# Stores of the attention rows on ScalarE's queue, loads at the head of a unit into three buffers, decay products ahead of the logits

## The chip, the core and the metric

One Trainium2 chip, one of its cores. The time of a kernel is the device time of one execution in microseconds (us); the median of the runs is compared. The profile names the engines PE (TensorE matmul), PEld (TensorE weight load), DVE (VectorE), ACT (ScalarE), POOL (GpSimd) and SP (SyncE). A name with a q behind it (SPq, ACTq) is that engine's instruction queue where it issues transfers.

## The reference, cut to what matters

Three stages follow one another: a gated recurrent attention, a mixture of experts with a greedy, capped assignment of tokens, and a two-layer network. The change touches the first alone.

```python
for t in range(S):                       # B, H, S, D = 4, 8, 768, 40
    m_new = np.maximum(f_gate[:, :, t] + m, i_gate[:, :, t])
    f_stab = np.exp(f_gate[:, :, t] + m - m_new)
    i_stab = np.exp(i_gate[:, :, t] - m_new)
    C = f_stab[..., None, None] * C + i_stab[..., None, None] * np.einsum('bhd,bhe->bhde', vt, kt)
    n = f_stab[..., None] * n + i_stab[..., None] * kt
    h_tilde = np.einsum('bhde,bhe->bhd', C, qt)
    denom = np.maximum(np.abs(np.einsum('bhd,bhd->bh', n, qt)[..., None]), 1.0)
    y[:, :, t] = h_tilde / denom / (1.0 + np.exp(-o_gate[:, :, t]))
x = y.transpose(0, 2, 1, 3).reshape(B * S, H * D)      # 3072 rows of 320
logits = x @ w_gate                      # then: greedy assignment of 3072 tokens to 8 experts
```

## The kernel before, in words

The sequence of 768 steps is cut into 12 chunks of 64 steps. A chunk holds four batches, taken as two pairs, so that the attention runs in 24 **units**: unit u is chunk n = u // 2 and batch pair bp = u % 2. The 128 partitions are 64 steps of the two batches of a pair. Inside a chunk the recurrence is written as matrix products with decay weights; from chunk to chunk a state (tile C, three buffers per pair) is carried.

For each chunk two transfers bring the inputs: `load_qk` (line 252) brings keys and queries (tile qk, 1 MB) into one of two fixed buffers, chunk n into buffer n % 2, and `load_vk` (line 256) brings values, keys by step and the output gate (tile vk, 968 KB), also into two buffers. Both are issued by SP. SP's queue also holds the stores of finished rows to device memory (xd, two stores of 64 rows for each unit, line 432) and the fetches of pieces of the later stage's weights (cx, line 856). It issues in the order of the program: an instruction that waits holds up all that stand behind it.

`run` (line 456) writes one unit after the other. In unit u, with v = u + 1 and w = u + 2, the work is:

- PE: `values(u)` and `scores(w)` interleaved (lines 368 and 283; the scores read qk of chunk w // 2), `recall(u)` and `state(u)` interleaved (382 and 394), `turn(u - 1)` (438, the transpose of finished rows), `logits(u - 1)` (448, it needs the transposed rows xT that ACT copies at 440), `decay(w)` (291, two times eight products into pF and pD).
- DVE: `scan(v)` (309) and `weigh(v)` (359), the denominators rd of `gates(u)` (414, 416, 418, once recall and state of unit u are done), `add_state(u)` (405), the finished rows x of `rows_out(u)` (427).
- POOL: sg (420, the gate times the reciprocal, it needs DVE's line 418), kt (328) and C (330) of `fade(v)`, vp (316) and qt (319) of `factors(v)`.
- ACT: xT (440), the sigmoid sg (354), the copy db of the second decay product (302), which qt reads, the logits L (449), and the last columns of x (429).

Between these, `fl(i)` puts steps of other work: the conversion of the weight pieces (lines 873 to 938, on ACT, DVE and POOL, from unit 4 on) and the first steps of the assignment of tokens (lines 608 to 628 on DVE, in one unit out of four).

In the kernel before, at the end of an even unit u, behind the stores of that unit, `load_qk` and `load_vk` of chunk u // 2 + 2 are issued. Their keys are first read by `scores` of unit u + 2. The last two units store through ACT's queue, the other 22 through SP's.

Of the kernel before, what the change touches and what calls it, by code (L numbers as in the profile page):

```python
# [8 lines left out]
F32 = mybir.dt.float32  # L9
# [8 lines left out]
NS, NU = 12, 24  # L18
# [16 lines left out]
class Plan:  # L35
# [46 lines left out]
    def next(self):  # L82
        self.due(min(self.todo)[0])
# [30 lines left out]
class Attention:  # L114
# [4 lines left out]
    def __init__(self, nc, tc, consts, qk, vk, ig, fg, wg, xd, L, ident):  # L119
        self.nc, self.tc, self.qk, self.vk, self.xd, self.L, self.ident = nc, tc, qk, vk, xd, L, ident  # L120
        self.es = ExitStack()
        one = self.es.enter_context(tc.tile_pool(name="a1", bufs=1))
# [19 lines left out]
        warm = one.tile([1, 8], F32, name="warm")  # L142
        V.memset(warm, 0.0)
        A.activation(warm, warm, AF.Exp)
        self.QKb = [one.tile([128, 2, 2, 8, 64], F32, name=f"qk{i}") for i in range(2)]
        self.QK, self.VK, self.W = {}, {}, {}
        for bp in range(2):
            self.load_qk(0, bp)
# [101 lines left out]
        self.nc.scalar.activation(self.isT[:, n0:n1].rearrange("p n h -> p (n h)"), self.pG[:, n0 * 16:n1 * 16], AF.Copy)  # L250

    def load_qk(self, n, bp=slice(0, 2)):
        self.QK[n] = self.QKb[n % 2]
        self.nc.sync.dma_start(self.QK[n][:, bp], self.qk[n, :, bp])

    def load_vk(self, n):
        self.VK[n] = self.two.tile([128, 2, 968], F32, name="vk")
        self.nc.sync.dma_start(self.VK[n], self.vk[n])

    def by_token(self, u, i):  # L260
# [161 lines left out]
    def rows_out(self, u):  # L422

        nc = self.nc
        n, bp = divmod(u, 2)
        x = self.st["x", u] = self.two.tile([128, 384], F32, name="x", bufs=3)
        nc.vector.tensor_tensor(x[:, :320].rearrange("p (h d) -> p h d", d=40), self.st.pop(("O", u))[:, :, :40],
                                self.st.pop(("sg", u)), op=ALU.mult)
        nc.scalar.activation(x[:, 320:], x[:, 256:320], AF.Copy)
        for r in range(2):  # L430
            row = (bp * 2 + 1 - r) * S + n * 64
            (nc.scalar if u > NU - 3 else nc.sync).dma_start(self.xd[row:row + 64], x[r * 64:r * 64 + 64])

    def turn(self, u):
        x = self.st.pop(("x", u))
# [20 lines left out]
    def run(self, hook, fill):  # L456
        later = self.later()
        for u in range(NU):
            v, w = u + 1, u + 2
            fl = lambda i: ([fill() for _ in range(FP[i])] if u > FU else []) + [self.step() for _ in range(EP[i])]  # L460
            self.both(self.values(u), self.scores(w))
            self.both(self.recall(u), self.state(u))
            if u > 0:
                self.turn(u - 1)
            if v < NU:
                self.scan(v)
                self.factors(v)
                self.opens(v)
                self.weigh(v)
            fl(0)  # L470
            if u < 3:
                next(later, None)
            self.gates(u, fl)
            if v < NU:
                self.fade(v)
            if u > 0:
                self.logits(u - 1)
            fl(2)
            if w < NU:
                self.decay(w)  # L480
            self.add_state(u)
            fl(3)
            if u == NU - 1:
                while self.extra:
                    self.step()
            self.rows_out(u)
            fl(4)
            if u % 2 == 0 and u // 2 + 2 < NS:
                self.load_qk(u // 2 + 2)
                self.load_vk(u // 2 + 2)  # L490
            if u == 0:
                self.turn_gi(2, NS)
                self.keep_gi(2, NS)
            hook(u)
        self.turn(u)
        self.logits(u)
        hook(NU)
        self.es.close()
# [1011 lines left out]
```

## Time and profile before

| what | value |
|---|---|
| median of 3 runs | 841.85 us (841.56 to 846.75) |
| the profiled execution's own time | 841.95 us |
| its span, first to last instruction | 840.2 us |
| stretch of the attention units (unit 0 to the last transpose) | about 16 to 187 us of the span |
| PE, DVE, ACT, POOL busy in the first 190 us | 132.8, 132.4, 66.9, 117.0 us |
| PE, DVE, ACT, POOL busy in the other 650.2 us | 597.4, 451.8, 282.8, 192.7 us |

The profiled execution lies 0.1 us above the median, and 1.75 us of its time lie outside its span. The share of an engine over the whole span says little here, as the attention and the later stages have different limits; each stage has to be read by itself.

### The profile page before, as it was taken

The numbers are of one execution on the slowest core, as the hardware profiler recorded it, in microseconds if no ns is written. First come the engines' busy times: TensorE is split into PE (matmuls) and PEld (weight loads), VectorE is DVE, ScalarE is ACT, GpSimd is POOL, SyncE is SP. The second block draws the span as 40 slices with busy tenths as digits, with TensorE's granted clock in tenths as the row PEclk, the third lists the DMA queues.
The fourth block names the chain that finished last, engine by engine and source line by source line (L and its number), as shares of the span: only waits on it lengthen the run. The fifth ranks groups of instructions, "written<-read, shape, count | busy, mean of one in ns | idle before, by whom it ended". The sixth has DMA issues, their size and how long they took to land.

```text
span 840.2 us, 18328 instructions
## 1 busy us (share of the span) xinstructions
PE 730.2 (87%) x7355; PEld 679.3 (81%) x7355; DVE 584.1 (70%) x1616; ACT 349.7 (42%) x743; POOL 309.7 (37%) x358
## 2 busy tenths in 40 slices
PE   7776667682889979989999999999999999999995
PEld 5665656571778878878988988899999999999995
DVE  8773776858788996688788778966942862662452
ACT  5322333333526652454354435424633643542431
POOL 3665776743622651352422414410601411211001
PEclk9765988895699989989999999999999999999998
DMA  5565565623520410220310301300310220100000
GB/s 206 182 245 169 164 261 174 221 54 110 181 63 19 149 64 25 84 83 1 128 62 3 112 17 63 104 24 2 128 40 24 91 76 25 63 1 25 1 1 24
DMA packets 20757, 72.79 MB, mean 87 GB/s; under 512 B 3200, under 2 KB 7296, under 8 KB 19264
## 3 DMA queue, kind: packets, MB, share of 16 engines
q1 hardware_dynamic: 11856, 39.41, 13.8%
q0 software_dynamic: 8448, 31.73, 11.4%
q8 instruction: 58, 0.95, 0.5%
q10 hardware_dynamic: 368, 0.49, 0.2%
q14 instruction: 27, 0.22, 0.1%
HBM read 62.96 MB, written 8.65 MB: 85 GB/s over the span
## 4 chain that ended last, share of the span: by engine, by line
PE 52%; DVE 16%; issue 6%; ACT 3%; DMA 0%; POOL 0%; POOLq 0%; ACTq 0%; DVEq 0%
PE ph L1096 24%; PE acc L1234 5%; PE acc L1238 4%; PE acc L1235 4%; PE acc L1203 3%; PE acc L1205 2%; PE acc L1204 2%; DVE e L1149 2%; PE pr L727 2%; DVE gl L980 1%; PE acc L1190 1%; DVE ge L713 1%; PE acc L1192 1%; PE ph L1049 1%; ACT e L1146 1%
## 5 line engine op out<-in xcount | busy, mean ns | idle before, releaser
L1234 PE MATMUL acc<-woh,gh 128*128 128x320 f32 x384 | 123.1, 321 | 0.0
L1238 PE MATMUL acc<-woh,gl 128*128 128x320 f32 x384 | 120.0, 312 | 0.0
L1235 PE MATMUL acc<-wol,gh 128*128 128x320 f32 x384 | 119.4, 311 | 0.0
L1149 DVE SCALAR_TENSOR_TENSOR e<-e,ph 128x384 f32<-128x384 f32 x128 | 69.8, 549 | 61.9 <-ACT e L1146 61.5
L1145 ACT ACTIVATE e<-ph 128x384 f32<-128x384 f32 x128 | 62.6, 489 | 117.4 <-PE ph L1096 113.0
L980 POOL TENSOR_TENSOR gl<-e,gh 128x384 fp32r<-128x384 f32 x33 | 34.4, 1045 | 165.2 <-DVE gh L974 129.9
L1096 PE MATMUL ph<-yh,wih 128*128 128x384 f32 x256 | 90.2, 352 | 0.4
L1096 PE MATMUL ph<-yh,wil 128*128 128x384 f32 x256 | 86.6, 338 | 0.0
L1113 ACT ACTIVATE gh<-ph 128x384 fp32r<-128x384 f32 x64 | 31.3, 491 | 123.0 <-PE ph L1096 121.8
L1244 POOL DMA_INDIRECT out_dram<-ot,idx x24 | 24.0, 998 | 141.3 <-ACT ot L972 138.0
L1120 DVE SCALAR_TENSOR_TENSOR gl<-ph,gh 128x384 fp32r<-128x384 f32 x64 | 35.3, 554 | 56.3 <-ACT gh L1113 55.9
L1238 PEld LDWEIGHTS acc<-woh,gl 128*128 128x128 f32 x384 | 72.8, 190 | 0.6
L1234 PEld LDWEIGHTS acc<-woh,gh 128*128 128x128 f32 x384 | 73.0, 190 | 0.2
L1235 PEld LDWEIGHTS acc<-wol,gh 128*128 128x128 f32 x384 | 73.0, 190 | 0.0
L1146 ACT ACTIVATE e<-e 128x384 f32<-128x384 f32 x128 | 67.3, 526 | 4.0
L1096 PE MATMUL ph<-yl,wih 128*128 128x384 f32 x256 | 66.8, 342 | 0.0
L283 PE MATMUL pS<-qk 64*64 64x64 f32 x768 | 37.5, 268 | 29.5 <-DMA qk<-in_qk_dram 29.5
L283 PEld LDWEIGHTS pS<-qk 64*64 64x64 f32 x768 | 33.5, 177 | 31.4 <-DMA qk<-in_qk_dram 31.4
L980 DVE TENSOR_TENSOR gl<-e,gh 128x384 fp32r<-128x384 f32 x95 | 57.3, 606 | 1.9
L1096 PEld LDWEIGHTS ph<-yh,wih 128*128 128x128 f32 x256 | 48.7, 190 | 4.5 <-ACT yh L1208 4.4
L1096 PEld LDWEIGHTS ph<-yh,wil 128*128 128x128 f32 x256 | 48.6, 190 | 0.0
L1096 PEld LDWEIGHTS ph<-yl,wih 128*128 128x128 f32 x256 | 46.6, 190 | 0.0
(269 smaller groups left out, 2033.2 us busy)
## 6 DMA issues: line engine op xcount, KB each, us to landing
vk<-in_vk_dram SPq DMA_DIRECT2D x12, 968.0 KB, 8.1
qk<-in_qk_dram SPq DMA_DIRECT2D x11, 1024.0 KB, 5.6
wx<-in_wout_dram SPq DMA_DIRECT2D x16, 320.0 KB, 2.8
xd<-x SPq DMA_DIRECT2D x44, 96.0 KB, 3.4
cx<-in_win_dram SPq DMA_DIRECT2D x8, 512.0 KB, 6.8
qk<-in_qk_dram SPq DMA_DIRECT2D x2, 512.0 KB, 5.4
cx<-in_win_dram SPq DMA_DIRECT2D x4, 256.0 KB, 6.2
xd<-x ACTq DMA_DIRECT2D x4, 96.0 KB, 2.2
```

The lines of the kernel that those rows point to most:

```text
L283: self.nc.tensor.matmul(p[r:r + 64, h], k, q, start=True, stop=True)
L980: (self.nc.vector if e == "d" else self.nc.gpsimd).tensor_tensor(out, x, y, op=ALU.subtract)
L1096: PE.matmul(p, w, x, start=k == 0, stop=k == 7)
L1113: nc.scalar.activation(h, p, AF.Relu)
L1120: nc.vector.scalar_tensor_tensor(l, p, 0.0, h, op0=ALU.max, op1=ALU.subtract)
L1145: nc.scalar.activation(e, p, AF.Relu, scale=-1.0)
L1146: nc.scalar.activation(e, e, AF.Exp, scale=-1.0)
L1149: nc.vector.scalar_tensor_tensor(e, e, -1.0, p, op0=ALU.add, op1=ALU.max)
L1203: PE.matmul(p, w[:, c], h, start=f == 0, stop=False)
L1234: PE.matmul(p, h[:, c], self.woh[:, f], start=f == 0, stop=False)
L1235: PE.matmul(p, h[:, c], self.wol[:, f], start=False, stop=False)
L1238: PE.matmul(p, l[:, c], self.woh[:, f], start=False, stop=f == 15)
```

## The change

Three things are done at once.

1. All row stores of the attention are issued by ACT instead of SP (44 of the 48 move; the other four were there).
2. The tiles qk and vk have three buffers, and the loads of chunk u // 2 + 2 are written at the head of the even unit u, ahead of its matmuls, instead of at its end.
3. `decay(w)` is written ahead of `logits(u - 1)`.

```diff
@@ __init__
-        self.QKb = [one.tile([128, 2, 2, 8, 64], F32, name=f"qk{i}") for i in range(2)]
+        self.QKb = [one.tile([128, 2, 2, 8, 64], F32, name=f"qk{i}") for i in range(3)]
@@ load_qk, load_vk
-        self.QK[n] = self.QKb[n % 2]
+        self.QK[n] = self.QKb[n % 3]
-        self.VK[n] = self.two.tile([128, 2, 968], F32, name="vk")
+        self.VK[n] = self.two.tile([128, 2, 968], F32, name="vk", bufs=3)
@@ rows_out
-            (nc.scalar if u > NU - 3 else nc.sync).dma_start(self.xd[row:row + 64], x[r * 64:r * 64 + 64])
+            nc.scalar.dma_start(self.xd[row:row + 64], x[r * 64:r * 64 + 64])
@@ run, for u in range(NU)
+            if u % 2 == 0 and u // 2 + 2 < NS:
+                self.load_qk(u // 2 + 2)
+                self.load_vk(u // 2 + 2)
             self.both(self.values(u), self.scores(w))
...
-            if u > 0:
-                self.logits(u - 1)
             fl(2)
             if w < NU:
                 self.decay(w)
+            if u > 0:
+                self.logits(u - 1)
             self.add_state(u)
...
-            if u % 2 == 0 and u // 2 + 2 < NS:
-                self.load_qk(u // 2 + 2)
-                self.load_vk(u // 2 + 2)
```

How the order of instructions moves at three places:

SP's queue around the loads of two chunks in the middle of the attention (xd is a row store, cx a piece of the later weights). Before:

```order
L254 DMA qk_109<-in_qk_dram 128x2048
L258 DMA vk<-in_vk_dram 128x1936
L856 DMA cx<-in_win_dram 128x1024
L432 DMA xd<-x 64x384 x4
L856 DMA cx<-in_win_dram 128x1024
L254 DMA qk_110<-in_qk_dram 128x2048
L258 DMA vk<-in_vk_dram 128x1936
```

With the change:

```order
L254 DMA qk_111<-in_qk_dram 128x2048
L258 DMA vk<-in_vk_dram 128x1936
L856 DMA cx<-in_win_dram 128x1024
L254 DMA qk_109<-in_qk_dram 128x2048
L258 DMA vk<-in_vk_dram 128x1936
L856 DMA cx<-in_win_dram 128x1024 x2
```

The four stores between two loads are gone from SP's queue, and a third buffer (qk_111) takes its turn; only loads and weight pieces are left.

PE from the transpose of one unit to the first products of the next one (pX holds the transpose and the logits, sel and fp, dp are the decay operands). Before:

```order
L438 MATMUL pX<-ident,x 128x128 x3
L448 MATMUL pX<-wg,xT 128x8 x3
L291 LDWEIGHTS sel
L291 MATMUL pF<-fp,sel 128x64
...
L291 MATMUL pD<-dp,sel 128x64
L368 MATMUL pO<-vp_121,P 64x64 x2
```

With the change:

```order
L438 MATMUL pX<-ident,x 128x128 x3
L291 LDWEIGHTS sel
L291 MATMUL pF<-fp,sel 128x64
...
L291 MATMUL pD<-dp,sel 128x64
L448 MATMUL pX<-wg,xT 128x8 x3
L368 MATMUL pO<-vp_121,P 64x64 x2
```

The sixteen decay products now stand between the transpose and the logits that wait for its copy.

ACT in one unit of the middle, with what each instruction waits for (DMAHW stands for a semaphore that a transfer raises when it has landed; eight of them take turns). Before:

```order
L440 ACTIVATE xT<-pX 128x384 [waits PE_49]
L354 ACTIVATE sg<-vk 128x320 [waits DMAHW0_49,Pool_49]
L449 ACTIVATE L<-pX 128x8 [waits PE_49]
L302 ACTIVATE db<-pD 128x512 [waits PE_49,Activation_49,Pool_49]
L868 ACTIVATE cg<-cx 128x512 [waits DMAHW3_49]
L429 ACTIVATE x<-x 128x64 [waits DMAHW6_49,DMAHW5_49,DVE_49]
```

With the change:

```order
L440 ACTIVATE xT<-pX 128x384 [waits PE_49]
L354 ACTIVATE sg<-vk 128x320 [waits DMAHW4_49,Pool_49]
L868 ACTIVATE cg<-cx 128x512 [waits DMAHW0_49]
L302 ACTIVATE db<-pD 128x512 [waits PE_49,Pool_49]
L449 ACTIVATE L<-pX 128x8 [waits PE_49]
L429 ACTIVATE x<-x 128x64 [waits DMAHW3_49,DVE_49]
L432 DMA xd<-x 64x384 [waits DMAHW5_49,Activation_49]
L432 DMA xd<-x 64x384 [waits DMAHW6_49]
```

The copy db now stands ahead of the logits L, and two stores stand behind x; each of the two also waits for an earlier transfer of its semaphore.

## Rows read from the trace of the kernel before

**Rows 1.** The page's first line: span and instructions.

```profile
span 840.2 us, 18328 instructions
```

**Rows 2.** Waits, 0 to 360 us: engine, line, waited for: us, times, longest.

```profile
PE pS L283 <- DMA qk<-in_qk_dram: 29.5, 10, 5.0
```

**Rows 3.** Waits, 31.3 to 169.9 us (units 2 to 19).

```profile
PE pS L283 <- DMA qk<-in_qk_dram: 27.6, 9, 5.0
POOL sg L420 <- DVE rd L418: 38.0, 13, 6.5
```

**Rows 4.** Timeline of SP's queue: start us, us, engine, line, operation, count.

```profile
108.17 8.18 SPq L432 DMA_DIRECT2D xd<-x  x4
...
118.03 0.37 SPq L254 DMA_DIRECT2D qk<-in_qk_dram  x1
```

**Rows 5.** The page's DMA issues: count, KB each, us from issue to landing.

```profile
vk<-in_vk_dram SPq DMA_DIRECT2D x12, 968.0 KB, 8.1
qk<-in_qk_dram SPq DMA_DIRECT2D x11, 1024.0 KB, 5.6
```

**Rows 6.** Timeline of PE; in brackets the idle time before a row.

```profile
117.44 0.93 PE L448 MATMUL pX<-wg,xT 128*128 128x8 f32 x6 [0.58 <-ACT xT L440]
...
124.05 0.37 PE L283 MATMUL pS<-qk 64*64 64x64 f32 x2 [4.84 <-DMA qk<-in_qk_dram]
```

**Rows 7.** Windows: us, busy per engine (instructions), granted clock, DMA share, GB/s.

```profile
31.30:169.90 138.60, 94.45 (x2759) 84.00 (x2756) 93.08 (x192) 46.35 (x114) 94.46 (x115) 0.80 0.58 199
60.00:74.00 14.00, 10.89 (x252) 9.47 (x247) 7.79 (x17) 3.14 (x9) 7.32 (x9) 0.51 0.38 113
124.00:126.00 2.00, 1.95 (x72) 1.95 (x76) 0.00 (x0) 0.00 (x0) 1.37 (x2) 0.50 0.97 397
```

**Rows 8.** Timeline of DVE, line 414, one row for each unit.

```profile
31.30 0.17 DVE L414 TENSOR_SCALAR rd<-pO 128x8 f32<-128x8 f32 x1 [0.95 <-PE pO L382]
...
111.79 0.17 DVE L414 TENSOR_SCALAR rd<-pO 128x8 f32<-128x8 f32 x1 [1.56 <-PE pO L382]
...
127.60 0.17 DVE L414 TENSOR_SCALAR rd<-pO 128x8 f32<-128x8 f32 x1 [3.62 <-PE pO L382]
...
142.24 0.17 DVE L414 TENSOR_SCALAR rd<-pO 128x8 f32<-128x8 f32 x1 [4.35 <-PE pO L382]
...
156.12 0.17 DVE L414 TENSOR_SCALAR rd<-pO 128x8 f32<-128x8 f32 x1 [1.61 <-PE pO L382]
...
169.86 0.17 DVE L414 TENSOR_SCALAR rd<-pO 128x8 f32<-128x8 f32 x1 [3.05 <-PE pO L382]
```

**Rows 9.** Timeline of POOL: gate products of four units, kt twice.

```profile
112.53 0.72 POOL L420 TENSOR_TENSOR sg<-sg,rd 128x320 f32<-128x320 f32 x1 [2.85 <-DVE rd L418]
...
119.20 0.72 POOL L420 TENSOR_TENSOR sg<-sg,rd 128x320 f32<-128x320 f32 x1 [1.19 <-DVE e L618]
...
128.34 0.72 POOL L420 TENSOR_TENSOR sg<-sg,rd 128x320 f32<-128x320 f32 x1 [2.97 <-DVE rd L418]
...
134.26 0.72 POOL L420 TENSOR_TENSOR sg<-sg,rd 128x320 f32<-128x320 f32 x1 [1.21 <-DVE rd L418]
...
144.14 0.73 POOL L328 TENSOR_TENSOR kt<-vk,W 128x320 f32<-128x320 f32 x1
...
149.93 1.19 POOL L328 TENSOR_TENSOR kt<-vk,W 128x320 f32<-128x320 f32 x1
```

**Rows 10.** Groups by line, POOL, 31.3 to 169.9 us: busy us, mean ns.

```profile
L328 POOL TENSOR_TENSOR kt<-vk,W 128x320 f32<-128x320 f32 x18 | 17.2, 957 | 0.0
L330 POOL TENSOR_TENSOR C<-C,db 128x328 f32<-128x328 f32 x18 | 17.0, 946 | 0.0
```

**Rows 11.** Timeline of ACT: transposed rows of two units, the last unit's stores.

```profile
65.61 0.49 ACT L440 ACTIVATE xT<-pX 128x384 f32<-128x384 f32 x1 [6.31 <-PE pX L438]
...
73.16 0.49 ACT L440 ACTIVATE xT<-pX 128x384 f32<-128x384 f32 x1 [3.63 <-PE pX L438]
...
185.51 1.10 ACTq L432 DMA_DIRECT2D xd<-x  x2
```

## The prediction, made before the changed kernel was run

> **What bounds the kernel now.** I read the busy time by stage first, because the change touches only the attention, some 170 of the 840.2 us [rows 1]. In the 138.6 us from unit 2 to unit 19 no engine is full: PE is busy 94.45 us, DVE 93.08, POOL 94.46, ACT 46.35 [rows 7]. Three engines stand at two thirds, so something makes all of them wait in turn. A unit takes 138.56 / 18 = 7.70 us (DVE's line 414 of unit 2 at 31.30, of unit 20 at 169.86) [rows 8].
>
> The waits name it. PE waits for the keys nine times in that stretch, 27.6 us in all, up to 5.0 us [rows 3]; with the time before unit 2 it is ten times and 29.5 us [rows 2]. POOL's 38.0 us of waiting for DVE's reciprocal [rows 3] and the idle time in front of DVE's line 414 (3.62, 4.35, 1.61, 3.05 us in the four even units 14, 16, 18 and 20) [rows 8] are the same delay handed on: denominators wait for PE's products, PE for keys.
>
> Why are the keys late? SP's timeline shows it: four stores occupy the queue from 108.17 for 8.18 us, since a store waits for its rows, and the load of the next keys is issued behind them at 118.03 [rows 4]. It needs 5.6 us to land [rows 5]; PE starts the products that read it at 124.05 after 4.84 us of idleness [rows 6]. So it is the moment of issue, not the rate. And the wait costs twice: the granted clock in the two us from 124 on is 0.50, the 1.2 GHz level [rows 7].
>
> **The change, part by part.**
>
> *Loads earlier.* At present a load is written at the end of unit 2n, behind that unit's stores, and first read at the head of unit 2n + 2: one unit of lead, less what the queue took. With three buffers the load of chunk n + 2 goes where chunk n - 1 lay, last read in unit 2n - 2. SP, with no stores left, can issue it between the end of unit 2n - 2 and the head of unit 2n. That is at least two units of lead, over 11 us, against 5.6 and 8.1 us to landing [rows 5]. The pieces of later weights stay in SP's queue; each waits for a buffer whose reader stands earlier in the program than the next load, so they can't push a load past the head of its unit. I take all ten waits for keys as gone.
>
> *What is late next.* Not all 27.6 us come back, and more than that may: the unit now follows DVE and POOL. I bound it from three sides.
> - Floor: POOL's 94.46 us of work without a gap, 5.25 us a unit [rows 7]. That saves 44.1 us. Against it, POOL and DVE hand work to each other in each unit (reciprocal to gate, gate to rows), so neither runs gapless.
> - DVE's own pace with the waits for late products cut out: from 111.79 to 169.86 eight units took 58.07 us, of which 3.62 + 4.35 + 1.61 + 3.05 = 12.63 us were such waits; 45.44 / 8 = 5.68 us a unit [rows 8]. Its other stalls are in that. It saves 36.3 us.
> - A unit as it ran without late keys on POOL, from one gate product to the next: 112.53 to 119.20 and 128.34 to 134.26, 6.67 and 5.92 us, each with 1.2 us of waiting for DVE inside [rows 9]. The slower one for all 18 units saves 138.6 - 120.1 = 18.5 us.
>
> I take 5.9 us a unit, the faster of those two units, which is also 0.2 above DVE's pace: 18 x 5.9 = 106.2, a saving of **32.4 us**.
>
> *Before unit 2 and after unit 19.* One wait, 29.5 - 27.6 = 1.9 us, lies before unit 2 [rows 2, 3]; the DVE is nearly full there, so I take 1 us of it, between 0 and 1.9. The load of chunk 2 now follows the first four at once and keeps the transfer engines busy for about as long as a load takes now, 5.6 to 8.1 us [rows 5], at a time in which nothing else needs them.
>
> *Decay ahead of the logits.* PE idles 0.58 us in each unit for the copy xT [rows 6]. The decay products now fill that gap, and ACT's copy db, which POOL's qt reads, comes earlier. While DVE and POOL set the pace this is worth nothing. In the last units, which carry no state, PE is near the bound: at most three times 0.58, 1.7 us, at least nothing; I take 1 us.
>
> *Stores on ACT.* Two stores cost ACT 1.10 us a unit [rows 11]. Its busy time is 46.35 / 18 = 2.6 us a unit, 3.7 with them, below 5.9. What queues behind them is the next unit's xT, and that waits for PE's transpose, which follows recall and state of that unit; these wait for POOL's kt and so begin some 0.7 us after the gate product, and end more than a us later. The stores cover the same time. I cost them at nothing; without that cover it would be up to 1.10 us in each of 22 units, 24 us.
>
> *Clock.* Pauses of 1 to 2 us remain in each unit. At 0.51 mean clock, between 60 and 74 us [rows 7], one unit took 73.16 - 65.61 = 7.55 us [rows 11], 1.65 above my pace. Most falls stood behind waits for keys; I keep two falls, 3.3 us, between none and nine (15 us).
>
> *Sum* against the profiled execution's 841.95 us (0.1 above the median of the runs): 841.95 - 32.4 - 1 - 1 + 3.3 = 810.9, so **811 us**. Everything behind the attention issues the same work in the same order, and I leave it as it is.
>
> *A rule that speaks against it.* POOL's kt took 0.73 us at 144.14 and 1.19 us at 149.93 [rows 9]; its mean is 957 ns, that of C 946 ns [rows 10]. DVE was busy beside both, so it depends on which of its operations runs. The Trainium skill, page "SBUF — State Buffer", section "Who interferes with whom", says that VectorE and GpSimd share a port pair as an exclusive lock: a VectorE operation with two SBUF inputs and a GpSimd operation that reads SBUF shut each other out. By it the squeeze makes such meetings more frequent. In numbers of rows: if every kt and C took 1.19 us, POOL would have 18 x (0.23 + 0.24) = 8.5 us more, and the sum would be 819 instead of 811. I leave the means, because the longest are already in the units that I measured.
>
> **Rivals.**
> - *The engines overlap better* (0.13): POOL's 94.46 us without gaps, two falls less: 841.95 - 44.1 - 2 = 796 us. For it: PE arrives without delay in every unit. Against it: 1.2 us of waiting in both units of [rows 9] that had their keys on time.
> - *DVE and POOL block each other, each unit like the slowest undelayed one* (0.14): 841.95 - 18.5 - 2 + 3.3 = 825 us. For it: 6.67 us in [rows 9], and the long kt.
> - *The low clock stays* (0.05): with the pauses spread, PE never returns to 2.4 GHz and a unit takes 7.55 us, or 6.97 without the 0.58 us wait: 838 or 827 us. Against it: at that level PE would have no pause left.
> - *The loads do not come earlier* (0.03): SP still waits, for a reader that ends late or for a semaphore: nothing gained, 842 us. The wait list of the order says that a load waits for PE and POOL, not how far they must be. Stores and loads also share engines: the Trainium skill, page "DMA: Bandwidth & Descriptors", section "Issuing engines are not separate DMA queues", says that issuing from several engines saves only issue time. What was lost here is issue time, the 8.18 us of [rows 4].
> - *Slower: ACT held by a semaphore* (0.03). Each store on ACT also waits for an earlier transfer of its semaphore, eight taking turns; with some seven transfers in two units that is often a load about two units (11.8 us) back. Once a load needs longer than that, ACT stands still, and behind it xT and db. If vk took twice its 8.1 us [rows 5], ACT would wait 16.2 - 11.8 = 4.4 us, with 2 x 1.10 us of issue on the path, 6.6 us in each of nine pairs of units: 9 x (11.8 + 6.6) = 165.6 against 138.6, 27 us more, 869 us. Against it: the landing times.
>
> **How the numbers follow.** The forecast has 0.62. The range of 798 to 827 holds it, the contention rival and the edge of two others, about 0.8. A difference of 1%, 8.4 us, is about what a measurement of this kernel can tell: faster than 833.5 us are the forecast, the first two rivals and half of the third (0.92); same are the rest of the third and the fourth (0.05); slower is the last (0.03).
>
> **What would show it.** In the profile after, PE's waits for keys are below 3 us in all; the span from unit 2 to unit 20 on DVE's line 414 is 102 to 112 us; POOL and DVE are near 90% busy in it, ACT near 45%, in which its stores do not count; the clock there is above 0.9; the later stages keep their 650 us. I am wrong if ACT shows waits for transfers in front of the stores, if kt and C lengthen past 1.1 us in the mean, if the clock stays low, or if a unit follows PE's waits for kt instead.

## The result: faster by 3.2%, 7 us above the forecast's sum

The changed kernel takes 817.89 us (median of 4 runs, 815.21 to 819.69), the kernel before, on the same chip, 844.3 us (841.56 to 847.47): a ratio of 0.968, 95% interval 0.963 to 0.974. The forecast was 811 us with a range of 798 to 827. Two executions with times far off the others, one of e9 (1352.04 us) and one of the kernel before (879.61 us, beside e1 to e4), are left out of all that follows. The profiled execution took 817.59 us, 0.3 below the median; its span is the first row of the page, which answers to [rows 1]:

```profile
span 815.8 us, 18330 instructions
```

The stretch from unit 2 to unit 20, on DVE's line 414, answers to [rows 8]. Start in us, duration, and in brackets the idle time before:

```profile
31.62 0.17 DVE L414 TENSOR_SCALAR rd<-pO 128x8 f32<-128x8 f32 x1 [1.46 <-PE pO L382]
40.23 0.17 DVE L414 TENSOR_SCALAR rd<-pO 128x8 f32<-128x8 f32 x1 [1.04 <-PE pC L394]
...
147.26 0.15 DVE L414 TENSOR_SCALAR rd<-pO 128x8 f32<-128x8 f32 x1
```

It lasts 115.64 us, 6.42 a unit, against 138.56 before: 22.9 us less. Unit 2 comes 0.3 us later than it did. Behind unit 20 the kernel takes 815.8 - 147.26 = 668.5 us against 670.3, 1.8 less. So 22.9 of the 24.4 us by which the span became shorter lie in the units.

Waits from 0 to 360 us, all that PE waited for keys and its longest unexplained groups; this answers to [rows 2] (us, times, longest):

```profile
PE pO L382 <- issue: 4.8, 3, 2.4
...
PE pC L394 <- issue: 4.1, 3, 2.4
...
PE pS L283 <- DMA qk<-in_qk_dram: 0.7, 1, 0.7
```

The ten waits for keys, 29.5 us, are gone; the one of 0.7 us that is left lies before unit 0. In their place "issue" appears: pauses in the middle of a run of products that no semaphore explains.

The windows answer to [rows 7]: the stretch, four of its units, and a pause at 28.6 us:

```profile
31.62:147.26 115.64, 95.36 (x2766) 87.90 (x2766) 95.00 (x191) 45.28 (x115) 93.81 (x115) 0.76 0.62 206
...
31.62:40.23 8.61, 6.87 (x155) 6.31 (x155) 3.46 (x9) 3.13 (x7) 7.02 (x22) 0.51 0.60 204
...
45.25:49.83 4.58, 4.04 (x156) 3.65 (x153) 4.51 (x10) 2.48 (x7) 3.39 (x5) 1.00 0.46 128
49.83:57.84 8.01, 5.58 (x147) 5.13 (x145) 7.97 (x16) 2.61 (x7) 7.42 (x7) 0.65 0.89 323
57.84:65.94 8.10, 7.41 (x158) 6.94 (x158) 4.17 (x10) 2.18 (x6) 5.52 (x6) 0.50 0.89 310
...
28.60:31.00 2.40, 0.03 (x3) 0.00 (x0) 1.47 (x2) 0.00 (x0) 0.00 (x0) 1.00 0.86 249
```

The reader should see two things. The work is the same as before (PE 95.36 us against 94.41, DVE 95.00 against 93.04, POOL 93.81 against 94.46) in a shorter time, so DVE is now 82% busy and POOL 81%. And the mean granted clock did not rise with the end of the waits: it is 0.76, before 0.80. Unit 2 ran wholly at the lower level (0.51 is 1.2 GHz) and took 8.6 us, unit 4 ran at 2.4 GHz and took 4.6; the two also differ in their work.

PE's timeline at three of the unexplained pauses:

```profile
31.01 0.25 PE L394 MATMUL pC<-vp,kt 64*40 64x64 f32 x1 [2.37 <-issue]
...
102.56 0.27 PE L382 MATMUL pO<-C,qt 64*64 64x64 f32 x1 [2.35 <-issue]
...
122.64 0.27 PE L382 MATMUL pO<-C,qt 64*64 64x64 f32 x1 [2.13 <-issue]
```

The clock was at 2.4 GHz up to the end of each pause, and behind each follows a stretch at 1.2 GHz. Windows of the second and third pause and of what follows them (their last three columns are again the granted clock, the DMA share and GB/s):

```profile
100.20:102.60 2.40, 0.05 (x2) 0.04 (x1) 1.19 (x2) 0.00 (x0) 2.40 (x3) 1.00 0.81 238
103.90:110.50 6.60, 6.58 (x154) 6.37 (x153) 5.98 (x14) 2.54 (x7) 4.95 (x5) 0.52 0.52 151
120.50:122.70 2.20, 0.07 (x5) 0.06 (x7) 1.22 (x2) 0.00 (x0) 2.20 (x3) 1.00 0.98 317
123.90:131.00 7.10, 6.99 (x160) 6.63 (x156) 5.54 (x16) 3.49 (x9) 4.56 (x6) 0.52 1.00 375
```

The loads now land later than those of [rows 5] did:

```profile
vk<-in_vk_dram SPq DMA_DIRECT2D x12, 968.0 KB, 8.7
qk<-in_qk_dram SPq DMA_DIRECT2D x11, 1024.0 KB, 8.0
```

POOL's groups in the stretch answer to [rows 10]:

```profile
L330 POOL TENSOR_TENSOR C<-C,db 128x328 f32<-128x328 f32 x18 | 16.6, 923 | 0.0
L328 POOL TENSOR_TENSOR kt<-vk,W 128x320 f32<-128x320 f32 x18 | 16.1, 896 | 0.0
```

Neither is longer than it was (946 and 957 ns).

### The profile page after: what moved, and what is told of

Its sections match the earlier page's. It is cut to its first block, busy times and chain, and to the rows that moved or that the text cites. A ratio compares the mean times of both kernels' runs of the same rounds, so it can differ in the third digit from the quotient of the medians.

```text
span 815.8 us, 18330 instructions
## 1 busy us (share of the span) xinstructions
PE 729.8 (89%) x7355; PEld 681.9 (84%) x7355; DVE 586.1 (72%) x1616; ACT 348.5 (43%) x743; POOL 309.2 (38%) x358
## 3 DMA queue, kind: packets, MB, share of 16 engines
q1 hardware_dynamic: 8336, 35.08, 12.6%
## 4 chain that ended last, share of the span: by engine, by line
PE 58%; DVE 21%; issue 8%; ACT 4%; DMA 4%; POOL 2%; ACTq 1%; SPq 0%; POOLq 0%; DVEq 0%
PE ph L1096 24%; PE acc L1234 5%; PE acc L1238 4%; PE acc L1235 4%; PE acc L1203 3%; PE acc L1205 3%; PE acc L1204 3%; DVE e L1149 2%; DMA xd<-x 2%; PE pr L727 2%; DVE ge L713 1%; DVE gl L980 1%; PE acc L1190 1%; PE pX L448 1%; DMA vk<-in_vk_dram 1%
## 5 line engine op out<-in xcount | busy, mean ns | idle before, releaser
L1113 ACT ACTIVATE gh<-ph 128x384 fp32r<-128x384 f32 x64 | 31.3, 491 | 121.9 <-PE ph L1096 120.7
L1096 PE MATMUL ph<-xh,w1h 128*128 128x384 f32 x128 | 45.0, 352 | 0.2
L1203 PE MATMUL acc<-gh,w 128*128 128x384 f32 x128 | 44.6, 349 | 0.0
```

What stands on the lines that cost most here:

```text
L1096: PE.matmul(p, w, x, start=k == 0, stop=k == 7)
L1113: nc.scalar.activation(h, p, AF.Relu)
L1203: PE.matmul(p, w[:, c], h, start=f == 0, stop=False)
```

## The experiments

What had to be told apart: which of the three parts brings the gain (e1 to e5), where the pauses come from (e6, e10, e12), whether the low clock can be held off (e7), and whether third buffers help or harm (e8, e9, e11). Times are medians; ratios are to the kernel before on the same chip. "Stretch" is unit 2 to unit 20 in the profiled execution, "pauses" are PE's idle times put down to "issue" from 10 to 165 us.

| kernel | ratio (95%) | us | unit 20 at | stretch | clock in it |
|---|---|---|---|---|---|
| change | 0.968 (0.963 to 0.974) | 817.89 | 147.26 | 115.64 | 0.76 |
| e1 stores on ACT | 0.974 (0.967 to 0.981) | 822.56 | 143.59 | 113.48 | 0.83 |
| e2 early loads, third buffers | 0.977 (0.971 to 0.982) | 826.98 | 154.78 | 124.68 | 0.74 |
| e3 decay ahead | 0.990 (0.986 to 0.993) | 840.17 | 165.83 | 134.66 | 0.76 |
| e4 e1 and e2 | 0.976 (0.969 to 0.983) | 827.19 | 152.86 | 121.41 | 0.76 |
| e5 e1 and e3 | 0.964 (0.960 to 0.967) | 813.99 | 142.18 | 111.93 | 0.85 |
| e6 change, no loads from chunk 3 | 0.958 (0.954 to 0.962) | 809.33 | 140.07 | 109.88 | 0.81 |
| e7 e5 and filler on PE | 0.977 (0.973 to 0.980) | 824.68 | 151.81 | 121.23 | 0.86 |
| e8 the change again | 0.970 (0.967 to 0.973) | 819.97 | 155.08 | 122.78 | 0.74 |
| e9 e5 and third buffers | 0.969 (0.964 to 0.974) | 820.7 | 149.99 | 118.00 | 0.75 |
| e10 e5 and 9 MB more | 0.976 (0.972 to 0.981) | 827.71 | 151.61 | 121.51 | 0.72 |
| e11 e5 again | 0.969 (0.964 to 0.974) | 820.27 | 143.09 | 112.98 | 0.77 |
| e12 e5 and 2 MB at the start | 0.969 (0.963 to 0.975) | 818.54 | 144.56 | 114.49 | 0.78 |

e1 to e4 ran together, e5 to e8, e9 to e11, and e12 alone; the kernel before took 848.95, 844.28, 847.34 and 844.02 us beside them, so the ratios are to be compared, not the times. The ratios are those on record, and not quotients of these medians; for e1 the medians would give 0.969 instead of 0.974. A profile is one execution; e8's is the slowest of its five runs (827.46 us), e9's also the slowest of those kept (827.22).

### e1: the stores alone

```diff
-            (nc.scalar if u > NU - 3 else nc.sync).dma_start(self.xd[row:row + 64], x[r * 64:r * 64 + 64])
+            nc.scalar.dma_start(self.xd[row:row + 64], x[r * 64:r * 64 + 64])
```

> Only the row stores move to ScalarE's queue; two buffers, loads at the end of the unit, logits ahead of decay. If what made the keys late was SyncE's queue standing at the stores, the loads now leave as soon as the last reader of their buffer is done, some 3 us before the unit's end: waits for keys fall from 29.5 us to 5 to 12 us, time 822 to 830 us. If the third buffer is what counts, the waits stay above 20 us and the time is 835 to 842 us. ScalarE's cost by itself: nothing seen, or up to 24 us if its queue is on the path.

All waits for keys in the units went, with two buffers and with the loads at the end of the unit; the 5 to 12 us that were expected to be left are not there. SP's queue, free of stores, issues each load as its buffer comes free. Three loads of keys in a row:

```profile
42.99 0.33 SPq L254 DMA_DIRECT2D qk<-in_qk_dram  x1
...
55.21 0.33 SPq L254 DMA_DIRECT2D qk<-in_qk_dram  x1
...
67.63 0.33 SPq L254 DMA_DIRECT2D qk<-in_qk_dram  x1
```

and POOL's qt, the last reader of the buffer that the second one fills:

```profile
53.92 1.26 POOL L319 TENSOR_TENSOR qt<-qk,db 128x512 f32<-128x512 f32 x1
```

It ends at 55.18 us and the load is issued at 55.21; the other two stand as close to theirs. So the load's place in the program no longer matters, since nothing else holds the queue. What made the keys late were the stores ahead of them.

### e2: early loads and third buffers alone

```diff
-        self.QKb = [one.tile([128, 2, 2, 8, 64], F32, name=f"qk{i}") for i in range(2)]
+        self.QKb = [one.tile([128, 2, 2, 8, 64], F32, name=f"qk{i}") for i in range(3)]
...
+            if u % 2 == 0 and u // 2 + 2 < NS:
+                self.load_qk(u // 2 + 2)
+                self.load_vk(u // 2 + 2)
             self.both(self.values(u), self.scores(w))
```

> Only the third buffers and the place of the loads at the head of the unit; stores stay on SyncE's queue, logits ahead of decay. The loads then stand behind the stores of one unit earlier, which still leaves nearly two units: waits for keys below 5 us, time 815 to 822 us. If the stores must leave the queue for the gain, 830 us or more.

The waits for keys went here too, but the time came out above the expected 815 to 822 us: the stretch took 124.68 us at a clock of 0.74. Stores and early loads are two cures for one illness; either is enough, and they don't add up.

### e3: decay ahead of the logits alone

```diff
             fl(2)
             if w < NU:
                 self.decay(w)
+            if u > 0:
+                self.logits(u - 1)
             self.add_state(u)
```

> Only the decay products ahead of the logits. With the keys still late the pace is theirs: 839 to 843 us. If TensorE's idle 0.58 us a unit were on the path, 24 x 0.58 = 14 us less, 828 us.

A gain of 1.05% (0.7 to 1.4), with the waits for keys still there, 39.0 us of them:

```profile
PE pS L283 <- DMA qk<-in_qk_dram: 39.0, 11, 6.7
```

The time of 840.17 us lies in the expected range only because the kernel before ran slowly beside it. The step was costed at 1 us, in the tail alone, and here it brings more. With the keys on time its gain is less sure: e1 to e5 and e4 to the change are pairs that differ by it alone, 0.974 to 0.964 and 0.976 to 0.968, but with the repeats of e5 and of the change (e11, 0.969, and e8, 0.970) the steps are 0.005 and 0.006, and those intervals overlap.

### e4: stores and early loads, without decay

```diff
-            if u > 0:
-                self.logits(u - 1)
             fl(2)
             if w < NU:
                 self.decay(w)
...
+            if u > 0:
+                self.logits(u - 1)
             fl(2)
             if w < NU:
                 self.decay(w)
```

(against the changed kernel.)

> The whole change without the decay products ahead of the logits. If VectorE and GpSimd set the pace of a unit, 816 to 820 us, as the whole change. If TensorE sets it in the units that it runs at its low clock, its idle 0.58 us in about ten of them and in the last ones come back: 822 to 826 us.

The time lies above both ranges, nearer to that of the theory that PE, at the lower clock, sets the pace in many units. PE's waits from 31 to 150 us show what the decay products fill. e4:

```profile
PE pX L448 <- ACT xT L440: 11.8, 18, 1.3
```

In the change that wait is 1.1 us in three. Some 11 us of gaps on PE are gone. The stretch is 5.8 us shorter (121.41 to 115.64), but a repeat of the change, e8, took 122.78, so the stretch does not show a gain.

### e5: stores and decay, without early loads

> The stores on ScalarE's queue and the decay products ahead of the logits, but two buffers and the loads at the end of the unit. If the early loads are worth something beside the stores, it is slower than the whole change: 822 to 828 us. If the stores alone had brought the keys on time, it equals the whole change or beats it: 812 to 818 us, with no waits for keys.

The edit is e1's and e3's together. Beside a repeat of the change (e8) it was the faster of the two: 813.99 against 819.97 us, with intervals that do not meet (0.960 to 0.967, 0.967 to 0.973). Its stretch:

```profile
30.25:142.18 111.93, 90.48 (x2759) 82.68 (x2759) 95.00 (x192) 44.53 (x113) 93.98 (x115) 0.85 0.74 245
```

and its loads land no later than those of [rows 5]:

```profile
vk<-in_vk_dram SPq DMA_DIRECT2D x12, 968.0 KB, 6.6
qk<-in_qk_dram SPq DMA_DIRECT2D x11, 1024.0 KB, 5.2
```

### e6: the change without 18 of its 24 loads

```diff
-            if u % 2 == 0 and u // 2 + 2 < NS:
+            if u == 0:
+                self.load_qk(2)
+                self.load_vk(2)
+            elif u % 2 == 0 and u // 2 + 2 < NS:
+                self.QK[u // 2 + 2], self.VK[u // 2 + 2] = self.QK[(u // 2 + 2) % 3], self.VK[(u // 2 + 2) % 3]
```

Chunks 3 to 11 read the inputs of chunks 0 to 2 again. Theory F, tested here: PE's instructions are themselves brought by transfers (the page lists a queue "q8 instruction" with 58 packets and 0.95 MB, in this kernel as in the one before), and behind big loads they come late, so PE pauses and its clock falls.

> The whole change, but chunks 3 to 11 read the inputs of chunks 0 to 2 again, so that 18 of the 24 large loads are left out (the result is another one). If TensorE's pauses that no semaphore explains come from transfers that its instructions stand behind, they fall from about 12 us to below 4 us in the attention, the clock rises above 0.85, and the stretch from unit 2 to unit 20 takes 106 us or less (from 115.6): 806 to 810 us. If VectorE and GpSimd hold the pace by themselves, the stretch stays at 112 us or more and the time at 814 to 818 us.

The time, 809.33 us, lies in the range of the first branch. Of PE's pauses none is left in front of a product; what PE waits for from 31 to 150 us is

```profile
PE pC L394 <- POOL kt L328: 14.1, 11, 2.1
...
PE pX L448 <- ACT xT L440: 1.3, 4, 0.6
```

and the stretch is the shortest of all:

```profile
30.19:140.07 109.88, 90.22 (x2755) 82.36 (x2754) 95.50 (x192) 44.90 (x114) 96.03 (x115) 0.81 0.28 74
```

So the later loads bring the pauses, and with loads and pauses 5.8 us go from the stretch of the profiled change. But it did not come down to 106 us, nor did the clock rise above 0.85: four units still ran below 0.60. What is left in front of PE's products are the waits for POOL's kt, one of the marks that the forecast named against itself.

### e7: filler on PE

```diff
+            if u > 2:
+                self.keep(10)      # ten products of 112 columns into a free part of pX
             self.both(self.recall(u), self.state(u))
```

(on e5.)

> The stores on ScalarE's queue and decay ahead of the logits, and in each unit from 3 on ten products of 112 columns more, into columns of pX that nobody reads, between the scores and the recall. If the low clock is what a unit loses, TensorE has no long pauses and stays at 2.4 GHz: clock above 0.9 in the stretch, 104 to 108 us for it, 805 to 811 us. If the low clock costs nothing because other engines set the pace, or if the ten products (0.5 us a unit at the high clock, 1 us at the low one) stand on the path, 816 to 828 us.

```profile
30.58:151.81 121.23, 100.75 (x2932) 90.72 (x2932) 91.89 (x193) 43.41 (x111) 94.19 (x115) 0.86 0.69 226
```

The clock was that of e5 (0.86, e5 0.85), though repeats of e5's program ran at 0.77 (e11) and 0.78 (e12, with 2 MB more), so whether the filler holds the clock up is not settled. PE got 10.3 us more to do, and the stretch grew by 9.3 us. In units with a clock of 0.9 or more it now takes 6.36 us (twelve of them), against 6.25 in e5. The filler costs what it takes and buys no time.

### e8: the change again

> The whole change once more, for a comparison on the same chip and beside the same runs: 814 to 820 us.

Its profile, at the slow end of its runs, has more time in pauses than any other (25.2 us, the change 12.6), among them 4.17 us in front of 114.06 and

```profile
130.41 0.36 PE L382 MATMUL pO<-C,qt 64*64 64x64 f32 x1 [4.68 <-issue]
```

With the windows of that pause and of the unit behind it:

```profile
125.70:130.40 4.70, 0.03 (x1) 0.00 (x0) 1.24 (x3) 0.00 (x0) 3.08 (x3) 0.71 1.01 377
130.90:136.00 5.10, 5.10 (x104) 4.89 (x102) 4.02 (x9) 2.33 (x6) 3.75 (x5) 0.50 0.70 241
```

PE stood still for 4.7 us with the transfer engines full, and then ran at 1.2 GHz. The same program took 115.64 us for the stretch in one execution and 122.78 in another.

### e9, e10, e11: third buffers, more bytes, and e5 once more

e9 is e5 with the third buffers, and with the loads still at the unit's end. e10 is e5 with

```diff
+        if n > 2:
+            self.nc.sync.dma_start(self.QKb[2], self.qk[n])
```

behind the load of vk, 1 MB for each of chunks 3 to 11 that nothing reads. e11 is e5 unchanged.

> Stores on ACT's queue, decay ahead of logits, and third buffers for qk and vk; the loads stay at the end of an even unit. Beside the change only the place of the loads differs; beside e5 only the buffers. If the third buffers do the harm (qk and vk of a chunk leave together and meet those of the chunk before), it is like e8: 817 to 823 us, vk landing in 8 us or more, PE's unexplained pauses above 14 us between 10 and 165 us. If the place does the harm (ahead of the weight pieces, which then bunch in SP's queue and hold the next loads back), it is like e5: 812 to 816 us, pauses below 13 us, clock above 0.82 in the stretch from unit 2 to unit 20.

> e5 with one more transfer of 1 MB behind the loads of each chunk from chunk 3 on, into a buffer that nothing reads; the work of the engines is the same. If PE's pauses come from transfers that fill the transfer engines (theory F), they grow with the bytes: from 12.5 us in e5 to 18 us or more, the clock in the stretch falls below 0.80 and the time is 820 to 828 us, with no new wait for keys. If the pauses do not hang on the amount of transfers, pauses and time stay as in e5: 812 to 816 us. A third way: the loads themselves now land late, and PE waits for qk again; then the waits for keys are above 3 us.

> e5 again, beside e9 and e10 on one chip: 812 to 816 us, 0.96 to 0.967 of the kernel before, if its first result was not chance; PE's unexplained pauses 10 to 14 us between 10 and 165 us. If e5's lead over the change was a lucky set of runs, it lands with the change at 817 to 822 us.

e9 met neither of its branches as a whole: its time (820.7 us) is that of the first, its pauses (10.5 us) those of the second; vk lands in 7.8 us and the clock is 0.75. As e11, which has no third buffers, has the same ratio on the same chip, the whole time shows no harm of the buffers. e11 did not repeat e5's 813.99 us: 820.27, ratio 0.969. Its stretch did repeat, 112.98 us against 111.93:

```profile
30.11:143.09 112.98, 96.02 (x2763) 88.81 (x2762) 92.69 (x192) 43.62 (x113) 94.10 (x115) 0.77 0.73 242
```

What was longer is the part behind unit 20: 818.6 - 143.09 = 675.5 us, where e5 had 670.4. e9 and e10, on the same chip, have 675.4 and 675.6 us there. So the ratio of e5 to the change rests on one set of runs; that e5 is not slower is shown twice, that it is faster only once.

e10 is 7.4 us above e11 (0.976 against 0.969), and each of its six runs is above each of e11's six. Its pauses are 18.9 us, 13.5 in e11, with no wait of PE's products for keys in the units:

```profile
30.10:151.61 121.51, 100.03 (x2759) 93.15 (x2759) 91.51 (x192) 44.04 (x113) 93.50 (x115) 0.72 0.86 302
```

More bytes, more pauses, a lower clock, and a longer stretch with the same work on DVE and POOL: that is what theory F expects. The times show it; the pauses alone would not, since two profiles of one program, the change and e8, differ by more (12.6 and 25.2 us).

### e12: 2 MB at the start

```diff
         self.load_vk(1)
+        nc.sync.dma_start(self.QKb[2], self.qk[2])
+        nc.sync.dma_start(one.tile([128, 2, 968], F32, name="vkx"), self.vk[2])
```

(on e5.)

> e5 with one thing more: two transfers of 1 MB and 968 KB, which nothing reads, behind the loads of chunk 1, where the third buffers let chunk 2's loads go. In the traces of the kernels with third buffers the transfer engines are 0.88 to 1.02 busy from 16 to 32 us, PE pauses for 1.6 to 2.9 us at about 31 us in front of a state product (line 394) that no semaphore holds, and unit 2 begins at 31.5 to 32.3 us; in e5 and e11 they are 0.3 to 0.6 busy, PE has no pause of over 0.9 us there, and unit 2 begins at 30.1 to 30.3. If the traffic makes the pause (theory F), it shows here too: a pause of 1.5 to 3 us at line 394 and unit 2 at 31.5 to 32.3 us, then units as in e5. If the pause belongs to the program of the three-buffer kernels (other places of loads, other waits), unit 2 begins at 30.1 to 30.3 as in e5. The whole time says little on 1.5 us: 0.963 to 0.971 of the kernel before either way.

A miss, and one that says little on the pause at 31 us: the added bytes were through by 24 us, and the spot that was aimed at stayed free.

```profile
16.00:24.00 8.00, 4.99 (x166) 4.64 (x166) 7.15 (x15) 3.81 (x9) 3.33 (x4) 1.00 0.95 376
24.00:28.00 4.00, 3.89 (x110) 3.72 (x108) 3.41 (x7) 2.91 (x7) 3.50 (x5) 0.60 0.32 121
```

Unit 2 began at 30.07 us, without a pause. But in the first window the transfer engines were as full as in the change and PE did not pause on its instructions there either. Full transfer engines alone are thus not enough. A count says the same: of the 78 pauses of 0.8 us or more in the profiles of the change and of e1 to e12 without e6 (25 to 165 us), 24 (31%) lie where the DMA share is 0.9 or more; of all two-us windows from 30 to 142 us, 257 of 672 (38%) do. But the share during a pause is the wrong place to look: what counts is the time before it, in which the next instructions should have come (below, "PE's pauses").

## Why the prediction was right, and where its sum was off

**The cause.** Right: the keys were late because their loads were issued late. e1 shows it more sharply than the forecast said it: the stores in SP's queue alone were the cause, and the larger lead of the third buffers was not needed.

**The pace without late keys.** I took 5.9 us a unit. In the profile after, the eight units whose granted clock is 0.90 or more take 5.89 us on average, so the term held. That it fits to 0.01 us is luck: such units average 5.35 us in e6 and 6.57 in e4, and within the change they go from 4.6 to 7.4.

**The clock.** This is the step that failed, by its number of falls. The price looked right: 7.55 us at the lower level, measured 7.44 us in the five units whose clock is below 0.60. But I kept two falls, 3.3 us, since most falls before stood behind waits for keys. After, five units are low throughout and five more in part (6.26 us on average): 5 x (7.44 - 5.9) + 5 x (6.26 - 5.9) = 9.5 us, 6.2 more than I kept, of the 6.7 us between the sum and the profiled execution. This adds up with 106.2 us to the stretch that was measured because it is that stretch, split by clock, and it is no clean price of the clock, as units differ in their work: unit 4 took 4.64 us at 1.00 in the change and 6.65 at 0.50 in e11, but unit 5 took 8.04 us at 0.65 in the change and at 1.00 in e5. The reason given for few falls was false: falls stand behind other pauses too. Four of the five low units follow a unit with one of the unexplained pauses, of 1.2 us or more, and for these the forecast had no term at all. e6, without them, took 109.88 us for the stretch, against 106.2 + 3.3 = 109.5 in the sum; that is one execution, and four of its units were still low, with neither late keys nor unexplained pauses.

**Before unit 2 and after unit 20.** I took 1 us for each. The head lost 0.3 us: PE's wait of 1.9 us before unit 2 went, but a pause of 2.37 us stands at 31.01. e1, e5, e11 and e12, with the stores on ACT and the loads of two buffers, reach unit 2 between 30.07 and 30.25 us. The tail gained 1.8. Together they miss by 0.5 us.

**Decay ahead of the logits.** Costed at nothing in the units, "while DVE and POOL set the pace". e3 puts it at 6 to 12 us in the kernel whose keys are late. So in some of its units DVE and POOL were not what the unit waited for. With the keys on time the pairs point the same way, but clear of noise only against e5's first set of runs. My reading, which no run tests by itself: where PE runs at the lower level it sets the pace, and then its wait for xT is on the path.

**Third buffers.** The forecast gave them the gain. The runs show none beside the stores on ACT: e5 without them is not slower than the change, and e9 has the ratio of e11. Alone, in e2, they cure the late keys as the stores do. The five profiles with three buffers and all loads reach unit 20 at 147.3 to 155.1 us, the four with stores on ACT and the loads of two buffers (e1, e5, e11, e12) at 142.2 to 144.6. Part of it is seen: loads of chunks 2 to 4 crowd the first 32 us, and from 24 to 28 us the DMA share is 0.95 in the change and 0.36 in e5, and from unit 1's line 414 to unit 3's it takes 16.4 to 17.3 us in the change, e8 and e9 against 13.7 to 13.8 in e1, e5 and e11 (15.1 in e4, but 13.7 in e2, whose stores hold the early loads back). The forecast took it that nothing else needs the transfer engines at that time; PE's own instructions do, and the pause of 2.37 us in front of 31.01 is a wait for them. The rest is not settled.

**Stores on ACT.** Costed at nothing. No run puts a price on them alone, but nothing contradicts it: e1 gains with them, and ACT is busy 47.21 of 113.48 us. One wait for a transfer in front of ACT's work is named in the stretch, apart from those in front of xT:

```profile
ACT x L429 <- DMA vk<-in_vk_dram: 0.4, 1, 0.4
...
ACT xT L440 <- DMA xd<-x: 7.4, 2, 5.2
```

The second row reads like the rival in which a semaphore holds ACT. Its longest entry, before xT at 104.82 us, is none: PE's transposes, which xT needs, ended at 104.8, after PE's pause in front of 102.56. A named transfer that came last by the records is not always what was waited for.

**Rivals.** That DVE and POOL block each other more is not borne out: kt and C became shorter, and POOL's busy time went from 94.46 to 93.81 us, though its product vp rose from a mean of 778 to 850 ns. The Trainium skill, page "SBUF — State Buffer", section "Who interferes with whom", has it that a VectorE operation with two SBUF inputs and a GpSimd operation that reads SBUF contend; the forecast took from it that the squeeze makes such meetings more frequent. The means here, 896 and 923 ns for kt and C, do not show that. "The low clock stays" was given 0.05; it stayed in five of eighteen units throughout and in five in part, and its mechanism, pauses spread over the units, is what was seen. (By its own terms its 838 us is 841.95 - 2.7 - 2 = 837.3.) Of the marks named ahead, the waits for keys and the later stages came true; the stretch of 102 to 112 us, DVE and POOL at 90%, ACT near 45% (45.28 of 115.64 us, 39%) and a clock above 0.9 did not. Of the signs of being wrong one came: the clock stayed low, 0.76 against 0.80. So the time fell into the range with the cause of the late keys right, but with the pace of the units behind it wrong in part.

**PE's pauses.** That the later loads bring them is shown by e6 and e10, and the traces show by which way. The queue "q8 instruction" moves packets of 16 KB, 58 in all for PE's 14710 products and weight loads, about one for each 256 (59 in e7, with 420 instructions more). Counted through PE's instructions in order, all 78 pauses and the two of the kernel before stand at one place, in front of the 194th or 195th of a block of 256, and each ends 1.2 to 1.7 us after such a packet has ended; in all fourteen profiles PE never passed this place sooner than 1.2 us after it. For the pause of the change in front of 102.56 us, the transfers from 100.1 to 101.3 us list

```profile
q8 instruction: 1, 0.02, 5.6%
```

and those from 101.3 to 102.6 us list none. The packet is late where the loads fill the transfer engines. From 25 to 165 us it begins at most 1.8 us after PE has passed the place of the block before in e6, but up to 6.4 us after it in the others; where it begins 3 us or more after it (85 times in thirteen profiles) the transfer engines are 0.91 busy in between, where it begins 0.3 to 1.5 us after it 0.33. In e12 a packet began 3.5 us after that place too, at 20.9 us, but PE, busy 4.99 of 8.00 us there, came to the next place 1.4 us after its end without a pause.

**What stays open.** How the 6 us between the sum and the measured stretch divide between the pauses themselves and the low clock behind them, what the decay products are worth when the keys are on time, and why the kernels with third buffers are later at unit 20 by more than the first units explain.

## What to carry to other kernels

When loads come late, look first at what stands ahead of them in their own queue: moving two stores to another engine's queue was one line and gave what two more buffers did, without putting more transfers at the start. Before a wait is costed as covered, ask at which clock the cover holds, and count units at each level in the trace instead of assuming that falls go with the wait that one removes. When PE pauses without a semaphore, look when the packets of its instructions landed: big loads that leave earlier can hold them back. When two executions of one program differ by 7 us in the same stretch, compare the stretch in several profiles before a variant is called better.

## What was not expected of the hardware

PE stops in the middle of a run of products, for 0.8 to 5.4 us, with no semaphore to explain it: 78 times in twelve profiles, never in the kernel without the later loads, and always at the place where the next 256 of its instructions have to be there. Two such pauses, of 3.4 us together, are in the kernel before.

Stores that ACT issues take 1.10 us a pair in 14 of 24 units of the change, but up to 1.96 us:

```profile
99.64 1.96 ACTq L432 DMA_DIRECT2D xd<-x  x2
```

Moving them bought SP's time at that price. The Trainium skill, page "DMA: Bandwidth & Descriptors", section "Issuing engines are not separate DMA queues", has it that a second issuing engine saves only the time that it takes to initiate the transfers. e1 agrees in that its program moves the same bytes, but what it won is more than that time. The 8.18 us of [rows 4], which the forecast called issue time, were mostly waiting: of the 138.6 us from unit 2 to unit 19 of the kernel before, SP's queue stood for 88.7 us at stores whose rows were not yet there.

```profile
SPq L432 <- ACT x L429: 88.7, 17, 10.1
```
